# Attention ahead of a mixture of experts: the turns of the queries and outputs a step later, the first twelve weight decodes in four pinned parts, a reordered start

## Chip, cores and metric

The kernel runs on one core of a Trainium2 chip. The metric is the device time of one execution in microseconds (us); the number to compare is the median of several runs. The engines are PE (matrix products, with PEld for its weight loads), DVE (vector), ACT (activation functions and copies), POOL (GpSimd) and SP, which here issues transfers (DMA).

## What is computed

Three stages follow one another; the change touches the first and the preparation of the second.

```python
def phi(x):                                # x: 8 batches, 8 heads, 576 rows, 64
    proj = np.einsum('bhsd,df->bhsf', x, w_phi)          # 128 features
    proj = proj - np.max(np.abs(proj), axis=-1, keepdims=True)
    return np.concatenate([np.exp(proj), np.exp(-proj)], axis=-1)
q_p, k_p = (phi(q), phi(k))
kv = np.einsum('bhsf,bhsd->bhfd', k_p, v)
z = np.sum(k_p, axis=2)
num = np.einsum('bhsf,bhfd->bhsd', q_p, kv)
den = np.einsum('bhsf,bhf->bhs', q_p, z)[..., None] + 1e-06
attn = num / den
h = x @ w_in                               # x: 4608 tokens x 512 from attn; 2048 hidden
x1 = (h * np.cos(h)) @ w_out
# then 8 experts, each token through the one of its largest logit (relu between w1 and w2)
```

The weights of the FFN (the second stage) arrive as 64-bit floats in two 32-bit words each, and the kernel itself turns a piece of 128 x 512 into 32-bit values: this is called a decode here.

## The kernel before

**Items and steps.** The attention works on 16 items (j = 0 to 15), each two batches by two heads. An item has five steps (m = 0 to 4), which cover 2, 2, 1, 2 and 2 blocks of 128 tokens of its rows. A step is written out as `turns(j,m)` and then `products(j,m)`, and runs as a software pipeline over two items: the projections belong to item j, the outputs to item j-1, the transposes of the loaded rows to item j+1.

**turns(j,m)** issues, on PE, the transposes `pt` of item j+1's rows (L110; ACT copies them to kT or qT, L113), the transposes `ptt` of the centred query features t_q of one step earlier (`qexp`, L178; ACT makes the two exponentials qx from them, L184), and the turn `po` of finished outputs xs of one step earlier, item j-1 (`outT`, L215; ACT copies them to xo, L217, and the last step of an item issues their transfer, L220). Then ACT makes the keys' exponentials ke (`kexp`, L142 and L143). At m = 1 and 2 the loads of later items are issued on SP's queue.

**products(j,m)** issues, on PE, the projections `pj` of queries and keys (L125), the outputs' numerators and denominators `pn` of item j-1 (`num`, L199), and the sums `kv` over the keys of two steps earlier (L163; at m = 4 ahead of pj). DVE then does, in this order of the code: m_q and t_q (the maximum and the difference, L130 and L131), rd (L204, L205) and xs (L206) of `num`, kvz (a copy of kv, L169, in some steps), m_k and t_k.

**What sets the order.** PE's instructions keep the written order (`keep`). DVE, ACT, POOL and SP are put in order by a scheduler, except for instructions that are kept in program order. `pj` has one tile of two banks; pt and ptt share two tiles, po and pn another two, kv two more.

**Decodes.** `moes` drives the attention as a generator with 170 stops, two per step, and calls other work between them; the stops 15 to 149 are run by one loop. In that loop a decode is called once per item, at n % 10 == 2 for items 3 to 14, which is m = 1: Abs on ACT (L398), four operations on DVE (L399, L400, L402, L403), a cast on ACT (L404), a subtraction on POOL (L408), and the staging transfer of the next piece into the single tile `sx` (L377 to L380). A scheduler is free to move these. Further decodes are called in the last 20 stops and in the FFN.

Of the kernel before, what the change touches and what calls it, by code (L numbers as in the profile page):

```python
# [11 lines left out]
F32 = mybir.dt.float32  # L12
# [3 lines left out]
AF = mybir.ActivationFunctionType  # L16
ALU = mybir.AluOpType
# [3 lines left out]
P = 128  # L21
# [4 lines left out]
F32_MAX = float.fromhex("0x1.dffffep-96")  # L26


def f32(ap):
    return ap.bitcast(F32)  # L30
# [13 lines left out]
def attention(tc, ctx, S, ps, ident, q, k, v, w_phi, xt):  # L44

    nc=tc.nc
    keep=tc.keep_in_program_order
    D=64; F=128; E1=D+1
    raw=ctx.enter_context(tc.tile_pool(name="a_raw",bufs=2))
    ap=ctx.enter_context(tc.tile_pool(name="a_sb",bufs=2))  # L50
# [1 line left out]
    pp=pctx.enter_context(tc.tile_pool(name="a_ps",bufs=1,space=PSUM))  # L52

    w2=ap.tile([P,F],F32,name="w2",bufs=1)
    for s in range(2): nc.sync.dma_start(w2[s*D:(s+1)*D,:],w_phi)
    nc.scalar.preload_act_table_set("natural_log_exp_and_others")

    items=[(bp,hp) for bp in range(4) for hp in range(4)]
    NI=len(items)
# [11 lines left out]
    def load_v(i):  # L71
        bp,hp=items[i]
        r=raw.tile([P,2,9,E1],F32,tag="vh",name=f"v_{i}")
        nc.gpsimd.memset(r[:,:,:,D:E1],1.0)
        for bb in range(2):
            s=v[2*bp+bb,2*hp:2*hp+2]
            for h in range(2):
                nc.sync.dma_start(r[:,h,5*bb:5*bb+4,0:D], s[h,0:512,:].rearrange("(p c) d -> p c d",c=4))
            nc.sync.dma_start(r[64*bb:64*bb+64,:,4,0:D], s[:,512:576,:].rearrange("h p d -> p h d"))
        return r  # L80

    raws={}
    def ld(t,i):
        if i<NI: raws[t,i]=load_v(i) if t=="v" else load(t,{"k":k,"q":q}[t],i)
# [3 lines left out]
    def block(r,b):  # L88
        r,r2=r
        if b==4: return r2.rearrange("p h d -> p (h d)")  # L90
        if b>4: b-=1
        j,h=b//2,b%2
        return r[:,h,2*j:2*j+2,:].rearrange("p c d -> p (c d)")
# [9 lines left out]
    def turn(i,m):  # L103
        pt=ps.tile([P,512],F32,tag="tr",name=f"pt_{i}_{m}")
        c=0; made=[]
        for t,c0,n in TURN[m]:
            if (t,i) not in T: T[t,i]=S("xT",f"{t}T_{i}")
            a=c
            for b in range(c0,c0+n):
                keep(nc.tensor.transpose(pt[:,c*P:(c+1)*P], block(raws[t,i],b), ident)); c+=1  # L110
            made.append((T[t,i][:,c0*P:(c0+n)*P],pt[:,a*P:c*P]))
        def vec():
            for x,p in made: nc.scalar.copy(x,p)  # L113
        return vec
# [72 lines left out]
    xss={}; xos={}  # L187
    def num(i,g):

        n=GR[g][1]; t0=GR[g][0]  # L190
        x=qx.pop((i,g))
        pn=ps.tile([P,512],F32,tag="nm",name=f"pn_{i}_{g}")
        for t in range(n):
            for h in range(2):
                o=pn[:,(2*t+h)*E1:(2*t+h+1)*E1]
                for sg in range(2):
                    for c in range(2):
                        bb=c if t0+t==4 else int(t0+t>4)
                        keep(nc.tensor.matmul(o[64*c:64*c+64],x[:,h,sg,t*P+64*c:t*P+64*c+64],kvs[i,bb][:,2*h+sg,:],start=sg==0,stop=sg==1,skip_group_check=True))  # L199
        pv=pn[:,:2*n*E1].rearrange("p (g d) -> p g d",d=E1)  # L200
        xs=xss[i,g]=ap.tile([P,256],F32,tag="xs",name=f"xs_{i}_{g}")
        def vec():
            r=ap.tile([P,4,1],F32,tag="rd",name=f"rd_{i}_{g}")[:,:2*n,:]
            nc.vector.tensor_scalar(r,pv[:,:,D:E1],1e-6,None,op0=ALU.add)  # L204
            nc.vector.reciprocal(r,r)  # L205
            nc.vector.tensor_tensor(xs[:,:n*P].rearrange("p (g d) -> p g d",d=D),pv[:,:,0:D],r.to_broadcast([P,2*n,D]),ALU.mult)  # L206
        return vec
# [15 lines left out]
    def at(j,m): return divmod(5*j+m,5)  # L223
    def turns(j,m):

        vecs=[]
        if j+1<NI: vecs.append(turn(j+1,m))
        i,g=at(j,m-1)
        if 0<=i<NI: vecs.append(qexp(i,g))
        i,g=at(j-1,m-1)  # L230
        if 0<=i<NI: vecs.append(outT(i,g))
        for f in vecs: f()
        i,g=at(j,m-1)
        if 0<=i<NI: kexp(i,g)
        if m==1:
            for t in "kq": ld(t,j+2)
        if m==2 and j>0: ld("v",j+1)
    def products(j,m):
# [11 lines left out]
        if todo and g==4: kvfin(i,1)  # L250
        if vk: vk()
        if j==NI-1 and m==4: pctx.close()
    for i in range(2):
        for t in "kqv": ld(t,i)
    for m in range(5): turn(0,m)()
    for j in range(NI+1):
        for m in range(5):
            turns(j,m)
            yield
            products(j,m)  # L260
            yield
    turns(NI+1,0)


def gate_consts(tc, ctx, cpool, ps, ident, modality_id, modality_bias, w_gate, wgt):
# [62 lines left out]
def moes(tc, ctx, consts, S, ps, ident, att, end_att, xt, w_in, w_out, x1d, tab, wgt, w1, w2, out):  # L328

    nc=tc.nc  # L330
# [3 lines left out]
    turns={}  # L334
    def turn(tags,what):

        n=turns.get(what,0); turns[what]=n+1
        return tags[n%len(tags)]
# [31 lines left out]
    def stage():  # L370

        x=next(sq,None)
        if x is None: return
        f,which=x
        a=stg(f"st_{f}_{which}")
        if which==0:
            nc.sync.dma_start(a.rearrange("p (c f) -> p c f",c=4),win64[:,:,f*P:(f+1)*P,:].rearrange("p c f w -> p c (f w)"))  # L377
        else:
            nc.sync.dma_start(a,wout64[f*P:(f+1)*P,:])
        st[f,which]=a  # L380
    decoded=[0]
    parts=[]
    def decode(paced=False):

        x=next(todo,None)
        if x is None: return
        decoded[0]+=1
        f,which=x
        v=st[f,which].rearrange("p (f w) -> p f w",w=2)
        H=v[:,:,1]; L=v[:,:,0]  # L390
        t=xtile("gl" if decoded[0]<=17 else "row",f"d_t{which}_{f}",F32)
        ti=t.bitcast(I32)
        h,l=pair(wtag[which][f],f"w{which}_{f}")
        (win,wout)[which][f]=(h,l)
        keep=tc.keep_in_program_order if paced else lambda ins: ins
        def one():

            nc.scalar.activation(t,H.bitcast(F32),AF.Abs,scale=2.0**-112)  # L398
            keep(nc.vector.tensor_scalar(t,t,F32_MAX,None,op0=ALU.min))  # L399
            keep(nc.vector.tensor_scalar(ti,ti,3,None,op0=ALU.logical_shift_left))  # L400
        def two():
            keep(nc.vector.scalar_tensor_tensor(ti,L,29,ti,op0=ALU.logical_shift_right,op1=ALU.bitwise_or))  # L402
            keep(nc.vector.scalar_tensor_tensor(ti,H,-0x80000000,ti,op0=ALU.bitwise_and,op1=ALU.bitwise_or))  # L403
            nc.scalar.copy(h,t)  # L404
            stage()
        def three():
            if paced: keep(nc.vector.tensor_tensor(l,t,f32(h),ALU.subtract))  # L407
            else: nc.gpsimd.tensor_tensor(l,t,f32(h),ALU.subtract)  # L408
        if paced: parts.append([one,two,three])
        else:  # L410
            one(); two(); three()
    def decode_part(n):
# [266 lines left out]
    def keep(ins):  # L679

        if pin: tc.keep_in_program_order(ins)
# [134 lines left out]
    for n in range(15,170-TAIL):  # L816
        next(att)

        if n%10==2 and 3<=n//10<15: decode()
    head={0:[lambda:load_x(0),stage],11:[lambda:split_x(0,0),lambda:split_x(0,1)],12:[lambda:split_x(0,2)],13:[lambda:split_x(0,3),lambda:step(0)],  # L820
          15:[lambda:step(1)],17:[lambda:step(2)]}
    for n in (1,5,10,12,15,17): head.setdefault(n,[]).append(lambda: decoded[0]<len(early) and decode())
# [171 lines left out]
```

## Time and profile before

| | us |
|---|---|
| median of 3 runs | 1741.84 |
| lowest and highest | 1739.44, 1741.93 |
| profiled execution | 1744.49 |
| its span | 1742.8 |
| mean granted clock of PE | 0.986 |

The profile is of one execution, whose own time lies 2.65 above the median and 1.7 above its span. Over the whole span PE is busy 94%, its weight loads 80%, DVE 66%, ACT 48%, POOL 24%. These shares are means over three unlike stages. The attention takes the first 415.69 us of the span, up to the first product of the FFN.

In the timelines a row starts with the time from the span's start, then the duration, the engine, the line of the code, the operation, what it writes and reads, and in brackets how long the engine had been idle and what ended that. Rows of several instructions of one kind are drawn together (x32).

### The profile page before, as it was taken

How to read it: one execution, taken by the hardware profiler on the slowest of the kernel's cores; microseconds unless marked ns; L12 is line 12 of the kernel's file. 1: busy time of each engine (PE TensorE's matmuls, PEld its weight loads, DVE VectorE, ACT ScalarE, POOL GpSimd, SP SyncE). 2: the span in 40 equal slices, each digit the busy share in tenths (PEclk: the TensorE clock that was granted, in tenths of full speed). 3: DMA queues.
4: the chain of work that ended last, by engine and by line, in shares of the span. 5: the costliest groups of instructions: out<-in, count | busy, mean ns of one | idle time of the engine just before them, and what ended most of it. 6: DMA issues, size and time to landing. Idle time of an engine off the chain costs nothing.

```text
span 1742.8 us, 33504 instructions
## 1 busy us (share of the span) xinstructions
PE 1637.3 (94%) x13058; PEld 1388.5 (80%) x13058; DVE 1144.7 (66%) x2332; ACT 830.5 (48%) x1529; POOL 426.4 (24%) x351
## 2 busy tenths in 40 slices
PE   6888999888979999999999999999799999999997
PEld 5777787777758888888888888878678999899976
DVE  3877666677886676768676868664556565655645
ACT  4566555555443343434343434344336565655645
POOL 0110000002232343433333334352321221211112
PEclk9999999999999999999999999999899999999999
DMA  6443333341321010101010101000358775766656
GB/s 182 139 152 116 101 111 97 106 130 54 111 86 64 13 37 12 38 7 43 7 43 7 43 7 43 7 1 25 122 158 330 238 241 183 250 226 218 224 182 211
DMA packets 142544, 190.06 MB, mean 109 GB/s; under 512 B 64535, under 2 KB 89239, under 8 KB 142370
## 3 DMA queue, kind: packets, MB, share of 16 engines
q1 hardware_dynamic: 134578, 166.74, 30.3%
q0 software_dynamic: 7792, 21.02, 3.6%
q8 instruction: 108, 1.77, 0.4%
q14 instruction: 66, 0.54, 0.1%
HBM read 157.98 MB, written 30.51 MB: 108 GB/s over the span
## 4 chain that ended last, share of the span: by engine, by line
PE 68%; DVE 16%; issue 6%; DMA 5%; ACT 3%; SPq 1%; POOL 1%; another core or an unknown queue 0%; DVEq 0%; POOLq 0%; ACTq 0%
PE ph L444 18%; PE acc L478 14%; PE mh L728 11%; PE po L740 10%; PE pj L125 4%; PE acc L483 4%; PE pn L199 2%; DMA tab<-rec,pi 2%; PE kv L163 2%; DVE m_q L130 1%; DVE t_q L131 1%; DVE t_k L131 1%; DVE d_t L403 1%; DVE m_k L130 1%; DVE x L434 1%
## 5 line engine op out<-in xcount | busy, mean ns | idle before, releaser
L444 PE MATMUL ph<-x,w 128*128 128x512 f32 x1728 | 424.0, 393 | 11.3 <-DVE fr L464 5.9
L444 PEld LDWEIGHTS ph<-x,w 128*128 128x128 f32 x1728 | 322.7, 188 | 87.1 <-DVE fr L464 8.2
L467 POOL TENSOR_TENSOR gl<-fr,gh 128x512 fp32r<-128x512 f32 x144 | 217.9, 1515 | 437.7 <-DVE gh L466 374.0
L688 DVE TENSOR_TENSOR m<-raw,m 128x512 fp32r<-128x512 f32 x320 | 210.3, 694 | 141.5 <-ACT m L687 141.0
L478 PE MATMUL acc<-w,gh 128*128 128x512 f32 x896 | 277.5, 391 | 1.9 <-DVE w L407 1.4
L687 ACT CAST m<-raw 128x512 fp32r<-128x512 f32 x320 | 187.0, 618 | 70.3 <-PE mh L728 33.6
L728 PEld LDWEIGHTS mh<-xT,m 128*128 128x128 f32 x1728 | 212.2, 194 | 7.1 <-DVE hl L731 3.7
L728 PE MATMUL mh<-xT,m 128*128 128x256 f32 x1728 | 213.3, 285 | 4.6 <-DVE hl L731 3.3
L457 ACT ACTIVATE n<-ph 128x512 int32<-128x512 f32 x144 | 85.8, 596 | 265.2 <-PE ph L444 264.8
L478 PEld LDWEIGHTS acc<-w,gh 128*128 128x128 f32 x896 | 169.0, 189 | 37.6 <-DVE w L407 1.7
L459 DVE SCALAR_TENSOR_TENSOR fr<-ph,n 128x512 f32<-128x512 f32 x144 | 99.1, 689 | 145.6 <-ACT n L457 131.6
L740 PE MATMUL po<-m,hh 128*128 128x512 f32 x576 | 181.3, 396 | 1.8 <-ACT hh L730 1.8
L508 DVE SCALAR_TENSOR_TENSOR junk<-x1T,wg 128x512 f32<-128x512 f32 x224 | 180.9, 808 | 0.0
L478 PE MATMUL acc<-w,gl 128*128 128x512 f32 x448 | 174.8, 390 | 0.0
L461 ACT ACTIVATE fr<-fr 128x512 f32<-128x512 f32 x144 | 91.1, 633 | 150.4 <-DVE fr L459 149.7
L464 DVE SCALAR_TENSOR_TENSOR fr<-fr,ph 128x512 f32<-128x512 f32 x144 | 98.7, 685 | 66.8 <-ACT fr L462 66.8
L740 PEld LDWEIGHTS po<-m,hh 128*128 128x128 f32 x576 | 106.0, 190 | 22.2 <-ACT hh L730 2.2
L778 POOL DMA_INDIRECT out_dram<-o,mrec x39 | 43.6, 1118 | 293.1 <-ACT o L777 284.8
L130 DVE TENSOR_REDUCE m_q<-pj 128x4 f32<-128x512 f32 (+1 forms) x80 | 50.9, 636 | 96.4 <-PE pj L125 96.4
L740 PE MATMUL po<-m,hl 128*128 128x512 f32 x288 | 113.1, 393 | 0.1
L478 PEld LDWEIGHTS acc<-w,gl 128*128 128x128 f32 x448 | 84.4, 188 | 17.7
L462 ACT ACTIVATE fr<-fr 128x512 f32<-128x512 f32 x144 | 91.0, 632 | 4.3
(189 smaller groups left out, 2364.9 us busy)
## 6 DMA issues: line engine op xcount, KB each, us to landing
raw<-in_moe_w_dram SPq DMA_DIRECT2D x171, 512.0 KB, 6.3
xt<-xo SPq DMA_DIRECT2D x16, 576.0 KB, 2.9
xr<-xt SPq DMA_DIRECT2D x36, 256.0 KB, 2.8
raw_k<-in_k_dram SPq DMA_DIRECT2D x32, 256.0 KB, 3.1
raw_q<-in_q_dram SPq DMA_DIRECT2D x32, 256.0 KB, 3.3
v<-in_v_dram SPq DMA_DIRECT2D x64, 128.0 KB, 3.0
st<-in_moe_w_in_dram SPq DMA_DIRECT2D x16, 512.0 KB, 3.7
st<-in_moe_w_out_dram SPq DMA_DIRECT2D x16, 512.0 KB, 3.6
```

Of the source, the lines that this page charges most:

```text
L444: nc.tensor.matmul(ph,A[:,ws],xhl[u,d][k],start=n[0]==0,stop=n[0]==11); n[0]+=1
L459: nc.vector.scalar_tensor_tensor(g,ph,INV2PI,n,op0=ALU.mult,op1=ALU.subtract)
L461: nc.scalar.activation(g,g,AF.Sin,scale=math.pi)
L462: nc.scalar.activation(g,g,AF.Square)
L464: nc.vector.scalar_tensor_tensor(g,g,-0.5,ph,op0=ALU.add,op1=ALU.mult)
L467: nc.gpsimd.tensor_tensor(gl,g,f32(gh),ALU.subtract)
L478: nc.tensor.matmul(accs[u][c],A[:,ws],B,start=(f==0 and k==0),stop=(f==NF-1 and k==2))
L508: return lambda: tc.keep_in_program_order(nc.vector.scalar_tensor_tensor(junk,x1T[u,c],1.0,wg[e],op0=ALU.mult,op1=ALU.mult,accum_out=lgs[u ...
L687: keep(nc.scalar.copy(h,a))
L688: keep(nc.vector.tensor_tensor(l,a,f32(h),ALU.subtract))
L728: nc.tensor.matmul(ph[:,f2*T:(f2+1)*T],A[:,ws],B[d//2][:,xs],start=n==0,stop=n==11); n+=1
L740: nc.tensor.matmul(po[c],A[:,ws],B,start=(f==0 and j==0),stop=(f==NF2-1 and j==2))
```

## The change

Four things are changed.

- `qexp` and `outT` are issued one step later: at step m they take what was made two steps earlier, not one. xs gets three buffers instead of two, and one more step of turns is added after the last item.
- The twelve decodes of the loop are cut into four parts, at the stops n, n+2, n+4 and n+6, which follow `turns(j,1)` to `turns(j,4)`. Each part has one operation of DVE, kept in program order: Abs and L415 in the first, L416, L417, then L418 with the cast, the staging transfer and POOL's subtraction.
- Item 1's first transposes are spread differently over item 0's steps: none at m = 0, then 0, 1, 2 with 3, and 4.
- The load of w_phi (w2) moves behind the first load of k.

```diff
@@ -52,7 +52,6 @@
     pp=pctx.enter_context(tc.tile_pool(name="a_ps",bufs=1,space=PSUM))
 
     w2=ap.tile([P,F],F32,name="w2",bufs=1)
-    for s in range(2): nc.sync.dma_start(w2[s*D:(s+1)*D,:],w_phi)
     nc.scalar.preload_act_table_set("natural_log_exp_and_others")
 
     items=[(bp,hp) for bp in range(4) for hp in range(4)]
@@ -198,7 +197,7 @@
                         bb=c if t0+t==4 else int(t0+t>4)
                         keep(nc.tensor.matmul(o[64*c:64*c+64],x[:,h,sg,t*P+64*c:t*P+64*c+64],kvs[i,bb][:,2*h+sg,:],start=sg==0,stop=sg==1,skip_group_check=True))
         pv=pn[:,:2*n*E1].rearrange("p (g d) -> p g d",d=E1)
-        xs=xss[i,g]=ap.tile([P,256],F32,tag="xs",name=f"xs_{i}_{g}")
+        xs=xss[i,g]=ap.tile([P,256],F32,tag="xs",name=f"xs_{i}_{g}",bufs=3)
         def vec():
             r=ap.tile([P,4,1],F32,tag="rd",name=f"rd_{i}_{g}")[:,:2*n,:]
             nc.vector.tensor_scalar(r,pv[:,:,D:E1],1e-6,None,op0=ALU.add)
@@ -224,10 +223,10 @@
     def turns(j,m):
 
         vecs=[]
-        if j+1<NI: vecs.append(turn(j+1,m))
-        i,g=at(j,m-1)
+        for n in ((),(0,),(1,),(2,3),(4,))[m] if j==0 else (m,) if j+1<NI else (): vecs.append(turn(j+1,n))
+        i,g=at(j,m-2)
         if 0<=i<NI: vecs.append(qexp(i,g))
-        i,g=at(j-1,m-1)
+        i,g=at(j-1,m-2)
         if 0<=i<NI: vecs.append(outT(i,g))
         for f in vecs: f()
         i,g=at(j,m-1)
@@ -250,8 +249,10 @@
         if todo and g==4: kvfin(i,1)
         if vk: vk()
         if j==NI-1 and m==4: pctx.close()
-    for i in range(2):
-        for t in "kqv": ld(t,i)
+    ld("k",0)
+    for s in range(2): nc.sync.dma_start(w2[s*D:(s+1)*D,:],w_phi)
+    ld("q",0); ld("v",0)
+    for t in "kqv": ld(t,1)
     for m in range(5): turn(0,m)()
     for j in range(NI+1):
         for m in range(5):
@@ -259,7 +260,7 @@
             yield
             products(j,m)
             yield
-    turns(NI+1,0)
+    for m in range(2): turns(NI+1,m)
 
 
 def gate_consts(tc, ctx, cpool, ps, ident, modality_id, modality_bias, w_gate, wgt):
@@ -381,6 +382,8 @@
     decoded=[0]
     parts=[]
     def decode(paced=False):
+        for _ in decoding(paced): pass
+    def decoding(paced=False,steps=False):
 
         x=next(todo,None)
         if x is None: return
@@ -406,7 +409,15 @@
         def three():
             if paced: keep(nc.vector.tensor_tensor(l,t,f32(h),ALU.subtract))
             else: nc.gpsimd.tensor_tensor(l,t,f32(h),ALU.subtract)
-        if paced: parts.append([one,two,three])
+        if steps:
+            keep=tc.keep_in_program_order
+            keep(nc.scalar.activation(t,H.bitcast(F32),AF.Abs,scale=2.0**-112))
+            yield keep(nc.vector.tensor_scalar(t,t,F32_MAX,None,op0=ALU.min))
+            yield keep(nc.vector.tensor_scalar(ti,ti,3,None,op0=ALU.logical_shift_left))
+            yield keep(nc.vector.scalar_tensor_tensor(ti,L,29,ti,op0=ALU.logical_shift_right,op1=ALU.bitwise_or))
+            keep(nc.vector.scalar_tensor_tensor(ti,H,-0x80000000,ti,op0=ALU.bitwise_and,op1=ALU.bitwise_or))
+            keep(nc.scalar.copy(h,t)); stage(); three()
+        elif paced: parts.append([one,two,three])
         else:
             one(); two(); three()
     def decode_part(n):
@@ -816,7 +827,8 @@
     for n in range(15,170-TAIL):
         next(att)
 
-        if n%10==2 and 3<=n//10<15: decode()
+        if n%10==2 and 3<=n//10<15: work=decoding(steps=True)
+        if n>=32 and n%2==0: next(work,None)
     head={0:[lambda:load_x(0),stage],11:[lambda:split_x(0,0),lambda:split_x(0,1)],12:[lambda:split_x(0,2)],13:[lambda:split_x(0,3),lambda:step(0)],
           15:[lambda:step(1)],17:[lambda:step(2)]}
     for n in (1,5,10,12,15,17): head.setdefault(n,[]).append(lambda: decoded[0]<len(early) and decode())
```

Line numbers after differ by one in the attention (L109, L124, L177, L198, L214 for L110, L125, L178, L199, L215); the parts of the decode are L414 to L419.

On PE, step (8,1), before: the names carry the item and the step (po_7_0 is the turn of xs of item 7, step 0).

```order
L110 MATMUL pt_9_1_3289<-ident_60,raw_k_9_2914 128x128 x4
L178 MATMUL ptt_8_0_3294<-ident_60,t_q_8_0_3239 128x128 x4
L215 MATMUL po_7_0_3301<-ident_60,xs_7_0_3262 128x128 x2
L125 MATMUL pj_8_1_3334<-w2_87,qT_8_2996 128x128 x4
L125 MATMUL pj_8_1_3334<-w2_87,kT_8_2815 128x128 x4
L199 MATMUL pn_7_1_3345<-kvz_7_0_3206,qx_7_1_3003 64x65 x16
```

The same step after:

```order
L109 MATMUL pt_9_1_3276<-ident_60,raw_k_9_2901 128x128 x4
L177 MATMUL ptt_7_4_3281<-ident_60,t_q_7_4_3163 128x128 x4
L214 MATMUL po_6_4_3287<-ident_60,xs_6_4_3186 128x128 x2
L124 MATMUL pj_8_1_3314<-w2_87,qT_8_2976 128x128 x4
L124 MATMUL pj_8_1_3314<-w2_87,kT_8_2803 128x128 x4
L198 MATMUL pn_7_1_3325<-kvz_7_0_3194,qx_7_1_3059 64x65 x16
```

The transposes ptt and the turn po of the step before have given place to those of two steps before; the projection pj_8_1 stands behind them as it did.

On DVE, step (1,4) before, with one of the twelve decodes (d_t0_2) in it:

```order
L169 COPY kvz_1_0_835<-kv_1_0_669 128x260
L399 TENSOR_SCALAR d_t0_2_2132<-d_t0_2_2132 128x512
L400 TENSOR_SCALAR d_t0_2_2132<-d_t0_2_2132 128x512
L130 TENSOR_REDUCE m_q_1_4_828<-pj_1_4_799 128x4
L402 SCALAR_TENSOR_TENSOR d_t0_2_2132<-st_2_0_1743,d_t0_2_2132 128x512
L131 TENSOR_TENSOR t_q_1_4_804<-pj_1_4_799,m_q_1_4_828 128x512
L204 TENSOR_SCALAR rd_0_4_831<-pn_0_4_810 128x4
L130 TENSOR_REDUCE m_k_1_4_837<-pj_1_4_799 128x4
L205 RECIPROCAL rd_0_4_831<-rd_0_4_831 128x4
L403 SCALAR_TENSOR_TENSOR d_t0_2_2132<-st_2_0_1743,d_t0_2_2132 128x512
L206 TENSOR_TENSOR xs_0_4_827<-pn_0_4_810,rd_0_4_831 128x256
L131 TENSOR_TENSOR t_k_1_4_809<-pj_1_4_799,m_k_1_4_837 128x512
```

The same kind of place after, step (8,1), with a first and a second part of a decode:

```order
L129 TENSOR_REDUCE m_q_8_1_3359<-pj_8_1_3314 128x4
L130 TENSOR_TENSOR t_q_8_1_3319<-pj_8_1_3314,m_q_8_1_3359 128x512
L415 TENSOR_SCALAR d_t0_4_3310<-d_t0_4_3310 128x512
L203 TENSOR_SCALAR rd_7_1_3362<-pn_7_1_3325 128x4
L129 TENSOR_REDUCE m_k_8_1_3368<-pj_8_1_3314 128x4
L204 RECIPROCAL rd_7_1_3362<-rd_7_1_3362 128x4
L168 COPY kvz_7_1_3366<-kv_7_1_3150 128x260
L205 TENSOR_TENSOR xs_7_1_3342<-pn_7_1_3325,rd_7_1_3362 128x256
L130 TENSOR_TENSOR t_k_8_1_3324<-pj_8_1_3314,m_k_8_1_3368 128x512
L416 TENSOR_SCALAR d_t0_4_3310<-d_t0_4_3310 128x512
```

Before, the scheduler put all four operations of a decode into one step of an early item, among m_q, t_q and xs. After the change, L415 stands between t_q and rd of the step (8,1), L416 behind its t_k, and the other two parts in the next two steps.

On PE, the start before:

```order
L110 MATMUL pt_0_4_156<-ident_60,raw_q_0_97 128x128 x4
L110 MATMUL pt_1_0_162<-ident_60,raw_k_1_111 128x128 x4
L125 MATMUL pj_0_0_169<-w2_87,qT_0_146 128x128 x4
L125 MATMUL pj_0_0_169<-w2_87,kT_0_132 128x128 x4
L110 MATMUL pt_1_1_186<-ident_60,raw_k_1_111 128x128 x4
L178 MATMUL ptt_0_0_191<-ident_60,t_q_0_0_174 128x128 x4
L125 MATMUL pj_0_1_215<-w2_87,qT_0_146 128x128 x4
```

And after:

```order
L109 MATMUL pt_0_4_156<-ident_60,raw_q_0_97 128x128 x4
L124 MATMUL pj_0_0_162<-w2_87,qT_0_146 128x128 x4
L124 MATMUL pj_0_0_162<-w2_87,kT_0_132 128x128 x4
L109 MATMUL pt_1_0_179<-ident_60,raw_k_1_111 128x128 x4
L124 MATMUL pj_0_1_201<-w2_87,qT_0_146 128x128 x4
L124 MATMUL pj_0_1_201<-w2_87,kT_0_132 128x128 x4
L109 MATMUL pt_1_1_218<-ident_60,raw_k_1_111 128x128 x4
L177 MATMUL ptt_0_0_223<-ident_60,t_q_0_0_167 128x128 x4
```

The first transposes of item 1 (pt_1_0) stood ahead of the first projection and now stand behind it; ptt_0_0 is a step later.

## Rows read from the trace of the kernel before

**Rows 1.** Windows: length, busy (count) of PE, PEld, DVE, ACT, POOL, PEclk, DMA, GB/s

```profile
100.00:125.00 25.00, 20.86 (x372) 18.09 (x372) 19.29 (x45) 17.00 (x37) 3.89 (x4) 0.95 0.53 157
200.00:250.00 50.00, 45.49 (x891) 39.70 (x891) 32.28 (x78) 28.57 (x66) 0.26 (x2) 1.00 0.37 107
```

**Rows 2.** Timeline, DVE, items 7 to 8: start, us, engine, line, operation [idle <-releaser]

```profile
201.09 0.69 DVE L130 TENSOR_REDUCE m_q<-pj 128x4 f32<-128x512 f32 x1 [1.70 <-PE pj L125]
...
205.40 0.43 DVE L130 TENSOR_REDUCE m_q<-pj 128x2 f32<-128x256 f32 x1 [0.90 <-PE pj L125]
...
214.79 0.69 DVE L130 TENSOR_REDUCE m_q<-pj 128x4 f32<-128x512 f32 x1 [0.54 <-PE pj L125]
...
219.69 0.69 DVE L130 TENSOR_REDUCE m_q<-pj 128x4 f32<-128x512 f32 x1 [1.70 <-PE pj L125]
...
221.88 0.69 DVE L131 TENSOR_TENSOR t_k<-pj,m_k 128x512 f32<-128x512 f32 x1
222.49 0.41 DVE L206 TENSOR_TENSOR xs<-pn,rd 128x256 f32<-128x256 f32 x1
224.59 0.69 DVE L130 TENSOR_REDUCE m_q<-pj 128x4 f32<-128x512 f32 x1 [1.69 <-PE pj L125]
```

**Rows 3.** Timeline, PE, the same place: two waits of the turned outputs

```profile
218.14 0.41 PE L215 MATMUL po<-ident,xs 128*128 128x128 f32 x2 [1.16 <-ACT qx L184]
...
223.05 0.41 PE L215 MATMUL po<-ident,xs 128*128 128x128 f32 x2 [0.36 <-DVE xs L206]
```

**Rows 4.** Timeline, PEld, one step: weight loads of each product

```profile
219.57 1.01 PEld L199 LDWEIGHTS pn<-kvz,qx 128*64 128x64 f32 x32
220.50 1.02 PEld L163 LDWEIGHTS kv<-v,ke 128*64 128x64 f32 x32
221.59 0.42 PEld L110 LDWEIGHTS pt<-ident,raw_k 128*128 128x128 f32 x4
221.98 0.47 PEld L178 LDWEIGHTS ptt<-ident,t_q 128*128 128x128 f32 x4
223.01 0.20 PEld L215 LDWEIGHTS po<-ident,xs 128*128 128x128 f32 x2 [0.57 <-ACT kT L113]
223.38 0.52 PEld L125 LDWEIGHTS pj<-w,qT 64*128 64x128 f32 x8 [0.17 <-issue]
```

**Rows 5.** Timeline, ACT: a decode's first operation in item 2; an exponential of (8,0)

```profile
88.92 0.67 ACT L398 ACTIVATE d_t<-st 128x512 f32<-128x512 f32 x1
...
224.51 0.65 ACT L143 ACTIVATE ke<-t_k 128x512 f32<-128x512 f32 x1
```

**Rows 6.** Timeline, DVE, the decode of item 2

```profile
89.63 0.43 DVE L399 TENSOR_SCALAR d_t<-d_t 128x512 f32<-128x512 f32 x1 [0.72 <-ACT d_t L398]
```

**Rows 7.** Timeline, PE, a wait behind that decode

```profile
92.46 0.63 PE L178 MATMUL ptt<-ident,t_q 128*128 128x128 f32 x4 [1.39 <-DVE rd L204]
```

**Rows 8.** Page, DMA issues: count, KB each, us to landing

```profile
st<-in_moe_w_in_dram SPq DMA_DIRECT2D x16, 512.0 KB, 3.7
```

**Rows 9.** Timeline, PE, start: first projection and the transposes ahead of it

```profile
14.64 1.08 PE L110 MATMUL pt<-ident,raw_k 128*128 128x128 f32 x4 [2.82 <-DMA raw_k<-in_k_dram]
15.65 1.23 PE L125 MATMUL pj<-w,qT 64*128 64x128 f32 x8
```

**Rows 10.** Timeline, DVE, first m_q of steps (0,0), (1,1), (2,0), (13,0), (15,0), (15,4)

```profile
17.78 0.69 DVE L130 TENSOR_REDUCE m_q<-pj 128x4 f32<-128x512 f32 x1 [14.94 <-PE pj L125]
...
47.42 0.69 DVE L130 TENSOR_REDUCE m_q<-pj 128x4 f32<-128x512 f32 x1
...
70.19 0.69 DVE L130 TENSOR_REDUCE m_q<-pj 128x4 f32<-128x512 f32 x1 [2.26 <-PE pj L125]
...
337.54 0.69 DVE L130 TENSOR_REDUCE m_q<-pj 128x4 f32<-128x512 f32 x1 [1.70 <-PE pj L125]
...
388.86 0.69 DVE L130 TENSOR_REDUCE m_q<-pj 128x4 f32<-128x512 f32 x1 [1.70 <-PE pj L125]
...
407.45 0.69 DVE L130 TENSOR_REDUCE m_q<-pj 128x4 f32<-128x512 f32 x1 [0.54 <-PE pj L125]
```

## Prediction

> **What bounds the kernel now.** I read the stretches of the span first, then the timelines of DVE, PE and the weight loads in one item of the attention, then the waits behind a decode, and last the start. The order of instructions differs only in the attention, which ends with the first product of the FFN about 416 us into the span, and in the ten microseconds behind it; everything after that stands as before. So the whole prediction is about the sixteen items of five steps each.
>
> In the quiet middle (items 5 to 11) no engine is full: of 50 us PE is busy 45.49, its weight loads 39.70, DVE 32.28, ACT 28.57, at clock 1.00 [rows 1]. The reader should see that the stretch is bounded by a loop and not by an engine. The loop shows when the starts of m_q are laid beside each other [rows 2]: step (8,0) begins at 219.69, its t_k ends at 221.88 + 0.69 = 222.57, its xs at 222.49 + 0.41 = 222.90, and only then, at 223.05, can PE turn that xs (po waits 0.36 for it, its weight load sat idle 0.57) [rows 3, 4]. The projection of the next step stands behind po on PE, begins at 223.38 [rows 4], and m_q of (8,1) follows 1.21 us later at 224.59 [rows 2]. PE thus waits for the last DVE operation of each step, and then DVE waits 1.69 for PE. One item takes 224.59 - 201.09 = 23.50 us [rows 2].
>
> **The moved turns.** After the change po turns, and ptt transposes, what DVE finished a whole step earlier, so neither has anything to wait for; the same instructions are issued as often as before. What still ties a step to the one before is that there is one tile pj: its products need t_k of the previous step to have read it. A step therefore takes the longer of two: PE's own work, or DVE from m_q to the end of t_k (2.88), the release (0.15, as from the end of xs to po), and projection to m_q (1.21), together 4.24. Since pj is single, the slack of one step can't be given to the next, and the item is the sum of the longer ones:
> - m = 0 to 1: 4.90 before; without the idle 0.57 it is 4.33, just over DVE's 4.24.
> - m = 1 to 2: 205.40 - 201.09 = 4.31. DVE also copies kvz here ahead of t_k, so DVE's chain is the longer one already; unchanged, 4.31.
> - m = 2 to 4: 214.79 - 205.40 = 9.39 for both. The wait before po of the second one (as long as in the first step) goes: 8.82. The one-token po and ptt move from the second to the first of the two, which shifts work between them and changes nothing in their sum.
> - m = 4 to 0: 219.69 - 214.79 = 4.90. Here po waited 1.16 [rows 3]; whichever ended last, the exponentials that the row names or xs, both are a step old afterwards. Without the wait PE has the shorter way, and DVE's 4.24 decides.
>
> Together 4.33 + 4.31 + 8.82 + 4.24 = 21.70 us, 1.80 less than 23.50. That a row names another releaser (the copy of kT for the idle weight load) does not matter here, since that copy too is older than po.
>
> **The decodes.** Items 2 to 14 take 388.86 - 70.19 = 318.67 us [rows 10], 13.2 more than 13 x 23.50 = 305.5; that excess is what decodes cost now. They stand at the wrong place: three to four DVE operations in one step, between m_q, t_q and xs, and PE behind them waits up to 1.39 [rows 7]. After the change each item from 3 to 14 has one decode, with one DVE operation in a step. Three of the four come behind t_k or xs, in time in which DVE would wait for pj (0.5 to 1.7 per step now [rows 2], less later), and I cost these at nothing; should that cover be gone, each costs at most its own duration, 0.4 to 0.7. The first one, L415, is pinned between t_q and rd of m = 1, hence ahead of t_k, in the step in which DVE's chain is the longer. It also waits for Abs on ACT, which stands behind the second exponential of the keys. That one ends at 224.51 + 0.65 = 225.16, Abs takes 0.67 and ends at 225.83 [rows 5]. With the quicker step m_q of (8,1) is at 224.02, t_q ends 1.42 later at 225.44: DVE waits about 0.4, and the operation takes 0.43 [rows 6], of which some 0.06 overlaps with its neighbours as all of DVE's rows do. That is 0.80 per decode, and 22.50 for such an item. Bounds: nothing, when Abs comes earlier and the operation is hidden, and 1.39, the longest wait behind a decode now. I stay near the middle because both durations come from rows.
>
> Items 13 and 14 hold four more decodes without pins: 388.86 - 337.54 = 51.32, or 4.3 over two quiet items [rows 10]. They are bunched up after the change by the order of DVE; I take 6, from 4 (as now) to 8 (twice).
> Items 2 to 14: 21.70 + 12 x 22.50 + 6 = 297.7, a gain of 21.0 (11.9 with 1.39 and 8; 32.6 with nothing and 4).
>
> **The start.** pj of (0,0) begins at 15.65 behind item 1's first transposes, which waited 2.82 for their load until 14.64 [rows 9]. Moved behind it, pj is free for as much as 3 us earlier. Later the constants' DVE work waits for its small loads, up to (1,1) at 47.42, and those loads are issued by SP in a row; much of the gain is lost there. Bounds 0 and 3.2, taken 2.0. From (1,1) to (2,0) it is 70.19 - 47.42 = 22.77 [rows 10]; without hoisted decodes it is 21.70 - 4.33 = 17.37, so 5.4 (3.5 if part of that is the loads). The load of w_phi now stands behind raw_k's first, still ahead of q, which pj needs in any case.
>
> **The end.** Item 15's first four steps take 407.45 - 388.86 = 18.59 [rows 10]. Without transposes of a next item (0.42 each [rows 4]) m = 2 to 4 is 8.82 - 0.84 = 7.98: 4.24 + 4.31 + 7.98 = 16.53, a gain of 2.1 (at least 1). One step of turns is added at the end and one wait for xs goes; with the FFN's first products behind it I take 0, up to 2 of gain.
>
> **Sum.** 2.0 + 5.4 + 21.0 + 2.1 = 30.5 us. The profiled run took 1744.49; so 1714.0 in its terms. That run is 2.65 above the median of 1741.84, so the median becomes 1711.3. The low bounds add to 16.4 (1725.4).
>
> **Rivals.**
> A. The pinned operation costs nothing (ACT is less than 60% busy [rows 1], so Abs may come early enough). Then 12 x 0.80 = 9.6 more: 1744.5 - 40.1 - 2.65 = 1701.7. Against it: the five ACT operations ahead of Abs run back to back after pt's end. Chance 0.10.
> B. The granted clock falls. While decodes were in the items it was 0.95 (100 to 125 us), in the middle, with its 1.16 waits once an item, 1.00 [rows 1, 3]. 0.95 means a tenth of the stretch at 1.2 GHz instead of 2.4 GHz, hence 2.5 of 25 us at half speed and 1.25 lost. If the one longer wait for L415 in each of twelve items does this, 1.15 x 12 = 13.8 goes: gain 16.7, time 1725.1. The same time comes if the wait for xs is merely replaced by that for t_k, which ends 0.33 earlier. Chance of either 0.17. [...]
> C. Slower: the pin turns a late load into a stall. L415 waits for Abs, Abs for the staging load (512 KB, 3.7 us to landing [rows 8]), which uses a single tile and is issued after the previous decode's last read, behind loads of q in SP's queue. DVE can no longer go round it: t_k, xs and then PE stand behind. This decides from 30.5 / 12 = 2.5 us per decode beyond the 0.80; with 4 us it is 48 lost, 1744.5 + 17.5 - 2.65 = 1759. Against it: from that last read to the next Abs there are at least two steps (4.24 + 4.33 = 8.6 us), some 4.9 more than the landing. Chance 0.06.
> D. Nothing changes: the waits of PE are replaced in full by equally long ones in the single pj. About 1742. Against it: DVE's 4.24 is from its own rows. Chance 0.04. Something between B and D 0.03.
>
> **How the numbers follow.** The forecast (gains of 25 to 36) has 0.60. The range takes in A, the low bounds and B: 1701 to 1728, leaving out 0.13. About 0.2% (3.5 us) is what a measurement of this kernel can tell from no change: faster 0.60 + 0.10 + 0.17 + 0.03 = 0.90, same 0.04, slower 0.06.
>
> **What would show it.** In the changed profile, quiet items 21.7 us long and those with a decode 22.5; po's waits for xs gone, and instead short waits of pj for t_k; L415 with a wait of about 0.4 for Abs and the rest of the decode hidden; (2,0) near 62.8; the FFN begins near 385. If po still waits, or items 5 to 11 are as long as now, the loop was not what I take it for; if L415 waits microseconds, it is C; if the clock is below 1.00 between 150 and 330 us, it is B.

## The result, and the profile after

The changed kernel takes 1710.3 us (median of 4, 1708.39 to 1711.51) against 1741.88 in the same set of runs: a ratio of 0.9818, 95% interval 0.9801 to 0.9835, 28.7 to 34.7 us faster. Forecast were 1711 and a gain of 30.5. The profiled execution took 1708.39, with a span of 1706.3.

The page of the changed kernel, its span and the busy time of PE and PEld:

```profile
span 1706.3 us, 33457 instructions
...
PE 1618.9 (95%) x13058; PEld 1384.3 (81%) x13058; DVE 1145.9 (67%) x2332; ACT 829.2 (49%) x1529; POOL 427.7 (25%) x351
```

The windows of after that answer to [rows 1] (length, busy time and count of PE, PEld, DVE, ACT, POOL, then clock, DMA share, GB/s):

```profile
100.00:125.00 25.00, 22.94 (x444) 20.84 (x442) 19.41 (x47) 16.35 (x39) 1.41 (x2) 1.00 0.43 122
200.00:250.00 50.00, 45.29 (x902) 40.96 (x900) 37.76 (x93) 33.58 (x77) 2.96 (x5) 1.00 0.46 140
```

The first stretch, which held hoisted decodes before, now has clock 1.00 and PE busy 22.94 instead of 20.86. In the second, which held none before and now holds about two, PE's own row hardly moves (45.29 against 45.49); the gain shows in its weight loads, 40.96 against 39.70. DVE's rise, 37.76 against 32.28, is mostly the decodes' own operations, which take 4.83 us there.

The timeline of DVE in items 8 and 9 after, the lines that answer to [rows 2]:

```profile
197.14 0.69 DVE L129 TENSOR_REDUCE m_q<-pj 128x4 f32<-128x512 f32 x1 [1.01 <-PE pj L124]
...
201.50 0.69 DVE L129 TENSOR_REDUCE m_q<-pj 128x4 f32<-128x512 f32 x1 [1.15 <-PE pj L124]
...
206.56 0.42 DVE L129 TENSOR_REDUCE m_q<-pj 128x2 f32<-128x256 f32 x1 [0.57 <-PE pj L124]
...
215.37 0.69 DVE L129 TENSOR_REDUCE m_q<-pj 128x4 f32<-128x512 f32 x1 [0.53 <-PE pj L124]
...
219.59 0.69 DVE L129 TENSOR_REDUCE m_q<-pj 128x4 f32<-128x512 f32 x1 [1.01 <-PE pj L124]
...
221.78 0.69 DVE L130 TENSOR_TENSOR t_k<-pj,m_k 128x512 f32<-128x512 f32 x1
...
223.95 0.69 DVE L129 TENSOR_REDUCE m_q<-pj 128x4 f32<-128x512 f32 x1 [1.15 <-PE pj L124]
...
225.68 0.43 DVE L415 TENSOR_SCALAR d_t<-d_t 128x512 f32<-128x512 f32 x1 [0.32 <-ACT d_t L414]
...
229.00 0.42 DVE L129 TENSOR_REDUCE m_q<-pj 128x2 f32<-128x256 f32 x1 [0.56 <-PE pj L124]
```

The starts of m_q give the steps of item 8: 4.36 from 197.14 to 201.50, 5.06 to 206.56, 8.81 for the two to 215.37, 4.22 to 219.59; 22.45 in all. L415 waited 0.32 for Abs and took 0.43, in the middle of the chain to t_k. On PE, at the start of item 9 (answering to [rows 3]):

```profile
218.39 0.72 PE L124 MATMUL pj<-w,qT 64*128 64x128 f32 x8 [0.74 <-DVE t_k L130]
...
222.43 0.38 PE L214 MATMUL po<-ident,xs 128*128 128x128 f32 x2
222.74 0.71 PE L124 MATMUL pj<-w,qT 64*128 64x128 f32 x8
...
226.56 0.38 PE L214 MATMUL po<-ident,xs 128*128 128x128 f32 x2
228.25 0.49 PE L124 MATMUL pj<-w,qT 64*128 64x128 f32 x4 [1.30 <-DVE t_k L130]
```

po has no wait any more, at 222.43 nor at 226.56. PE waits at pj instead, for t_k: 0.74 at m = 4 to 0, 1.30 at m = 1 to 2, and not at all in the other steps (pj at 222.74 follows po at once). The waits between 100 and 300 us (engine, line, for what: us in total, times, longest) have no row of po left:

```profile
DVE m_q L129 <- PE pj L124: 40.3, 44, 1.4
...
PE pj L124 <- DVE t_k L130: 18.4, 18, 1.3
...
DVE d_t L415 <- ACT d_t L414: 2.8, 9, 0.3
```

The starts of the same steps as in [rows 10]: (0,0), (1,1), (2,0), (13,0), (15,0), (15,4):

```profile
14.09 0.69 DVE L129 TENSOR_REDUCE m_q<-pj 128x4 f32<-128x512 f32 x1 [11.25 <-PE pj L124]
...
45.59 0.68 DVE L129 TENSOR_REDUCE m_q<-pj 128x4 f32<-128x512 f32 x1
...
63.17 0.69 DVE L129 TENSOR_REDUCE m_q<-pj 128x4 f32<-128x512 f32 x1 [1.01 <-PE pj L124]
...
309.38 0.69 DVE L129 TENSOR_REDUCE m_q<-pj 128x4 f32<-128x512 f32 x1 [1.01 <-PE pj L124]
...
357.16 0.68 DVE L129 TENSOR_REDUCE m_q<-pj 128x4 f32<-128x512 f32 x1
...
374.89 0.69 DVE L129 TENSOR_REDUCE m_q<-pj 128x4 f32<-128x512 f32 x1 [0.54 <-PE pj L124]
```

### The profile page after: what moved, and what is told of

Read it like the earlier page. It is cut to its first block, busy times and chain, and to the rows that moved or that the text cites. A ratio compares the mean times of both kernels' runs of the same rounds, so it can differ in the third digit from the quotient of the medians.

```text
span 1706.3 us, 33457 instructions
## 1 busy us (share of the span) xinstructions
PE 1618.9 (95%) x13058; PEld 1384.3 (81%) x13058; DVE 1145.9 (67%) x2332; ACT 829.2 (49%) x1529; POOL 427.7 (25%) x351
## 4 chain that ended last, share of the span: by engine, by line
PE 72%; DVE 13%; issue 5%; DMA 5%; ACT 4%; SPq 1%; POOL 1%; another core or an unknown queue 0%; DVEq 0%; POOLq 0%; ACTq 0%
PE ph L455 19%; PE acc L489 15%; PE mh L739 11%; PE po L751 10%; PE acc L494 4%; PE pj L124 3%; PE kv L162 3%; PE pn L198 2%; DMA tab<-rec,pi 2%; PE pt L109 2%; DVE x L445 1%; DMA raw<-in_moe_w_dram 1%; DVE t_k L130 1%; DVE d_t L406 1%; DVE m_k L129 1%
```

## The experiments

Each kernel below is timed beside the kernel before on the same chip; a ratio is to that. Differences between two of them come from these ratios, and the intervals of the single ratios are 4 to 11 us wide, so the step lengths of the traces, which in regular items repeat within 0.02 almost everywhere, tell more than the totals. They are differences of the starts of m_q, here of a regular item between 6 and 10:

| kernel | 0 to 1 | 1 to 2 | 2 to 4 | 4 to 0 | item | time, us | ratio (95%) |
|---|---|---|---|---|---|---|---|
| before | 4.90 | 4.31 | 9.39 | 4.91 | 23.51 | 1741.9 | 1 |
| after | 4.36 | 5.06 | 8.81 | 4.22 | 22.45 | 1710.3 | 0.9818 (0.9801-0.9835) |
| turns_only | 4.36 | 4.31 | 8.81 | 4.23 | 21.71 | 1717.1 | 0.9840 (0.9824-0.9857) |
| parts_only | 4.91 | 5.09 | 9.29 | 4.91 | 24.20 | 1738.5 | 0.9962 (0.9949-0.9975) |
| outt_only | 4.36 | 5.06 | 8.81 | 4.22 | 22.45 | 1711.4 | 0.9798 (0.9775-0.9822) |
| qexp_only | 4.90 | 5.11 | 9.51 | 4.90 | 24.42 | 1742.3 | 0.9984 (0.9973-0.9995) |
| late415 | 4.36 | 4.31 | 8.81 | 4.22 | 21.70 | 1700.8 | 0.9754 (0.9726-0.9783) |
| tkfirst | 4.36 | 4.47 | 8.81 | 4.22 | 21.87 | 1702.7 | 0.9763 (0.9737-0.9789) |
| late_tkall | 4.36 | 3.79 | 8.82 | 4.15 | 21.12 | 1692.9 | 0.9701 (0.9670-0.9733) |
| late_tkall_tail | 4.36 | 3.79 | 8.82 | 4.15 | 21.12 | 1689.4 | 0.9690 (0.9663-0.9717) |
| quad415 | 4.37 | 6.25 | 8.81 | 4.22 | 23.65 | 1728.4 | 0.9921 (0.9899-0.9943) |

**The parts of the change, one at a time.** The theory is that of the prediction; the first rival holds the decodes' places to be the larger part.

> The kernel before with the two moves of turns alone; decodes free and bunched in early items as before, start as before. Theory: items without decodes 21.7 us instead of 23.5 (items 6 to 12), the bunched ones keep their excess of about 9 us; gain 1.8 x 14.5 = 26 less what bunched decodes take back, time 1716 to 1722. Rival (the decodes' places are the larger part): 1730 or more.

The quiet items came out at 21.70 to 21.71, all the gain of the loop without the rest of the change, and the time in the range given. Items 1 to 5, in which the scheduler still put the decodes, took 27.28, 25.07, 26.98, 27.04 and 23.15.

> The kernel before with the twelve pinned decodes alone. Theory: quiet items stay at 23.5, an item with a decode about 24.3 since L415 lies in DVE's chain at m = 1 too; it wins the excess of the bunched decodes (about 14 over items 1 to 4) and pays 0.8 to 1.2 twelve times: gain 0 to 5, time 1737 to 1742. Rival (bunching was the larger part): gain over 10, 1731 or less.

The pinned decodes alone win 6.6 us (0.38%), a little more than expected. Items 3 to 13 are 24.2 long: L415 costs 0.8 in the step 1 to 2 with the old turns as with the new, and the other three operations cost nothing (the other steps are as long as before or 0.1 shorter). The two ratios fall by 0.0160 and 0.0038; the change as a whole by 0.0182. The moved turns are the larger part; whether the parts add up to the whole can't be told within these intervals.

**Which of the two turns.** The changed kernel with one of the two put back to its old place, so that the other alone is a step later:

```diff
         # outt_only
-        i,g=at(j,m-2)
+        i,g=at(j,m-1)
         if 0<=i<NI: vecs.append(qexp(i,g))
```

```diff
         # qexp_only
-        i,g=at(j-1,m-2)
+        i,g=at(j-1,m-1)
         if 0<=i<NI: vecs.append(outT(i,g))
```

> The changed kernel, but the transposes of the queries' features (qexp) stay one step back as before; only the turned outputs (outT) are moved. Theory (the wait of po for xs, at the end of DVE's step, held the loop): the whole gain stays, items with a decode 22.5 us, items without 21.7, time about 1710. Rival (the exponentials were what po and the products waited for): the 1.16 wait at m = 4 to 0 stays, item 23.1 or more, time about 1720.

> The changed kernel, but the turned outputs (outT) stay one step back as before; only qexp is moved. Theory: po waits for xs again, 0.57 and 0.57 and 0.7 more per item, item with a decode 24.3 us, time about 1737 (1710 + 15 x 1.8). Rival (the exponentials held the loop): half or more of the gain stays, 1724 or less.

With outT alone every item from 2 on is as long as with both (within 0.02); with qexp alone the loop is the old one (24.42 beside the 24.20 of parts_only). In qexp_only's waits between 100 and 300 us po stands as before, behind xs in 16 of its steps, by its row behind the exponentials in 8, and by its row behind the copy of qT in 8 more:

```profile
PE po L214 <- DVE xs L205: 10.7, 16, 1.0
PE po L214 <- ACT qx L183: 10.3, 8, 1.3
...
PE po L214 <- ACT qT L112: 4.0, 8, 0.5
```

In outt_only, whose exponentials stand where they were, all three rows are gone, and PE has only its wait for t_k:

```profile
DVE m_q L129 <- PE pj L124: 38.5, 44, 1.2
...
PE pj L124 <- DVE t_k L130: 17.3, 18, 1.3
```

So the row that named the exponentials (the 1.16 of [rows 3]) was not about them: leaving them in place and moving xs ended the wait. The time of qexp_only lies 5 above what was expected; its item 14, with decodes that the scheduler bunched there, took 28.48 us, against 24.37 before.

**L415, and what stands ahead of t_k.** late415 moves L415 to the next part; tkfirst writes t_k ahead of the output's operations at m = 1; late_tkall does both, the second in every step:

```diff
-            yield keep(nc.vector.tensor_scalar(t,t,F32_MAX,None,op0=ALU.min))
-            yield keep(nc.vector.tensor_scalar(ti,ti,3,None,op0=ALU.logical_shift_left))
+            yield
+            yield keep(nc.vector.tensor_scalar(t,t,F32_MAX,None,op0=ALU.min))
+            keep(nc.vector.tensor_scalar(ti,ti,3,None,op0=ALU.logical_shift_left))
...
         if vq: vq()
+        if vk: vk()
         if vn: vn()
         if todo and g==2: kvfin(i,0)
         if todo and g==4: kvfin(i,1)
-        if vk: vk()
```

> The changed kernel with the first DVE operation of each decode taken out of the chain of m = 1: Abs alone in the first part, L415's operation one part later (behind t_k), the next two together, the last as it was. Theory: step 1 to 2 falls from 5.05 to 4.31, 0.74 x 12 = 8.9 less than the changed kernel, about 1701.5. Rival (DVE's work as such costs the time, wherever it stands): other steps grow by as much, about 1710.

> The changed kernel with t_k written ahead of kvz and xs at m = 1 only. Theory (t_k frees the single pj, so what stands ahead of it is paid in full): kvz (0.31) and xs (0.33) leave the chain, step 1 to 2 falls by 0.64 in some 15 items, 9.5 in all, about 1701. Rival (the step is held by PE, or xs late now holds pn): unchanged, about 1710.

> Both at once, and t_k ahead of rd, kvz and xs in every step. Theory: the step 1 to 2 becomes PE's (about 3.75), 4 to 0 loses about 0.1; item with a decode 22.45 - 1.30 - 0.1 = 21.0, about 20 less than the changed kernel, 1690. Rival (the freed time is taken by the next wait, xs for pn or ACT's copies): half of it, 1700.

The step 1 to 2 fell to 4.31 in late415, to the number, and in items 3 to 13 no other step grew. Item 14, with the bunch of decodes that have no pins, did: 27.32 there and 27.06 in tkfirst, against 25.34 in the changed kernel. In tkfirst the step 1 to 2 fell by 0.59 of the 0.64 expected. With both it is 3.79, with no wait of PE in it, and the item 21.12 instead of 21.0; the one wait of PE that is left is 0.67 in the step 4 to 0. DVE in late_tkall_tail, from m_q to the next m_q, step (7,1):

```profile
172.89 0.69 DVE L129 TENSOR_REDUCE m_q<-pj 128x4 f32<-128x512 f32 x1 [0.80 <-PE pj L124]
...
174.22 0.68 DVE L129 TENSOR_REDUCE m_k<-pj 128x4 f32<-128x512 f32 x1
...
175.00 0.69 DVE L130 TENSOR_TENSOR t_k<-pj,m_k 128x512 f32<-128x512 f32 x1
...
175.70 0.40 DVE L168 COPY kvz<-kv 128x260 f32<-128x260 f32 x1
176.01 0.41 DVE L205 TENSOR_TENSOR xs<-pn,rd 128x256 f32<-128x256 f32 x1
176.34 0.41 DVE L416 TENSOR_SCALAR d_t<-d_t 128x512 f32<-128x512 f32 x1
176.67 0.42 DVE L129 TENSOR_REDUCE m_q<-pj 128x2 f32<-128x256 f32 x1
```

t_k starts 2.11 after m_q, where after L415, kvz and xs it started 3.47 after it (227.42 against 223.95 in the changed kernel). kvz, xs and the decode's operation now lie in the time in which PE works on.

> The same, and the decodes behind the twelve (the last twenty stops) also cut in parts, one per stop, instead of left to the scheduler, which bunched five of them in items 14 and 15. Theory: items 14 and 15 lose their excess of 2.9 + 1.2, 3 to 4 less than without, 1687. Rival (the FFN's first products then wait for their weights): the gain is given back, 1690 or more.

In the changed kernel the decodes behind the twelve (L402 to L406) stand together in items 14 and 15, beside the last pinned one, and DVE has no wait left there (changed kernel, DVE, around the steps (14,2) and (14,3)):

```profile
340.59 0.75 DVE L402 TENSOR_SCALAR d_t<-d_t 128x512 f32<-128x512 f32 x2
341.26 0.42 DVE L403 TENSOR_SCALAR d_t<-d_t 128x512 int32<-128x512 int32 x1
341.60 0.41 DVE L129 TENSOR_REDUCE m_q<-pj 128x2 f32<-128x256 f32 x1
...
343.91 0.68 DVE L405 SCALAR_TENSOR_TENSOR d_t<-st,d_t 128x512 int32<-128x512 int32 x1
...
344.85 0.68 DVE L406 SCALAR_TENSOR_TENSOR d_t<-st,d_t 128x512 int32<-128x512 int32 x1
...
346.05 0.68 DVE L129 TENSOR_REDUCE m_q<-pj 128x4 f32<-128x512 f32 x1
```

Item 14 takes 25.34 there and 25.15 in late_tkall; with the late decodes cut in parts it takes 21.12, like the others. These decodes now stand in item 15 and behind it, and the excess of item 15 stays: its first four steps take 17.84, against 17.53 in late_tkall. The medians fell by 3.5, near what was expected, the ratios by 0.0011 (1.9 us); their intervals overlap, so the totals neither show the gain nor exclude the rival. PE of late_tkall_tail is busy 193 of 200 us and its loads 175, at clock 1.00:

```profile
100.00:300.00 200.00, 193.06 (x3827) 175.28 (x3825) 164.45 (x385) 137.53 (x311) 13.92 (x19) 1.00 0.48 139
```

This is the fastest version but for best_nest below, which can't be told from it: 0.9690 of the time before, 22 us below the changed kernel by the ratios (0.9818 - 0.9690, times 1742).

**The start.**

oldstart puts item 1's first transposes and the load of w_phi back; nest keeps the zeros' tiles while the constants are made:

```diff
         # oldstart
-        for n in ((),(0,),(1,),(2,3),(4,))[m] if j==0 else (m,) if j+1<NI else (): vecs.append(turn(j+1,n))
+        if j+1<NI: vecs.append(turn(j+1,m))
...
         # nest
-        return gate_consts(tc, ctx, cpool, ps, ident, modality_id, modality_bias, w_gate, wgt)
+            return gate_consts(tc, ctx, cpool, ps, ident, modality_id, modality_bias, w_gate, wgt)
```

> The changed kernel with the start as before: item 1's first transposes in their old places, w_phi loaded first. Theory of the prediction: the reordered start is worth about 2 of the 7.4 us that step (2,0) gained, so (2,0) comes near 65 instead of 63.2, time 1712. Rival (the constants' DVE work, which becomes ready at 39.5 in both traces, takes back the whole gain of the start): (0,0) at 17.8, but (2,0) within 0.5 of 63.2, time 1710.

(0,0) begins at 17.83 and (2,0) at 66.75, 3.6 later than in the changed kernel, and the FFN at 386.4 instead of 382.8. So the reordered start is worth 3.6 there, more than expected, and the rival is out. The total (0.9793, 0.9769 to 0.9818) doesn't show it: the two ratios' intervals overlap, and from the first ph, the FFN's first product, to the first mh, the experts' first, the profiled executions of the nine kernels with the same order of instructions there differ by up to 2.6 us (829.8 to 832.4; 830.8 after, 829.9 here). What the start is worth in the total stays open.

> The changed kernel with the tiles of the gate's constants in space of their own, instead of in the space of the zeros whose four transfers land at 39.2. Theory: POOL's first constant waits for these transfers to leave the space, DVE's casts wait for POOL, and t_q of (1,0) stands behind them (3.4 idle); without that (1,0) goes on at once and the small loads are issued some 4 us earlier, so (2,0) comes 3 to 5 earlier, at 58 to 60, time about 1706. Rival (item 1 is held by the loads for items 1 and 2 in SP's row): (2,0) stays within 1 of 63.2, time 1710.

Where the start's gain is lost is seen in the changed kernel at 35 to 41 us. On POOL the constants wait for the zeros to leave the space that they take over:

```profile
39.23 0.21 POOL L288 MEMSET tf<- 128x128 f32 x1 [36.06 <-DMA x1d<-zero]
```

and on DVE t_q stands behind the casts of these constants, 4.2 behind its m_q:

```profile
35.48 0.69 DVE L129 TENSOR_REDUCE m_q<-pj 128x4 f32<-128x512 f32 x1 [1.35 <-PE pj L124]
39.55 0.17 DVE L294 CAST rev<-ri 128x8 f32<-128x8 int32 x1 [3.38 <-POOL ri L293]
...
39.72 0.68 DVE L130 TENSOR_TENSOR t_q<-pj,m_q 128x512 f32<-128x512 f32 x1
```

nest took that wait away, and the step (1,1) came a microsecond earlier, at 44.56, but (2,0) came at 63.43: the theory's price was wrong. The rival's number came true, but its reason, the loads in SP's row, is not shown by that. On PE the time was lost again (nest, PE):

```profile
48.11 0.49 PE L124 MATMUL pj<-w,qT 64*128 64x128 f32 x4 [2.47 <-DVE t_k L130]
...
48.75 1.14 PE L198 MATMUL pn<-kvz,qx 128*64 128x65 f32 x16
49.67 1.95 PE L162 MATMUL kv<-v,ke 128*64 128x65 f32 x32
```

PE had waited 2.47 for t_k, and the rows after it are at the lower clock: pn 1.14 for 16 products where 0.69 is usual, kv 1.95 where it is 1.10. The granted clock was 0.78 between 50 and 55 us. The changed kernel has such a wait one step earlier, with the lower clock behind it (granted 0.73 between 40 and 45 us). Its row names g, a DVE operation that ends 0.1 behind t_k:

```profile
42.36 1.22 PE L124 MATMUL pj<-w,qT 64*128 64x128 f32 x8 [2.30 <-DVE g L279]
```

There nest waits 0.48 and its clock is 1.00. It thus moved the wait and the fall one step on: its PE is 2.9 ahead at the next transposes (44.07 against 46.98) and level at the ones after (51.55 against 51.58). The total is 1706.9 (0.9785, 0.9762 to 0.9807), which can't be told from the changed kernel.

> The fastest so far (t_k first in every step, L415 out of the chain, the late decodes in parts) with the constants in space of their own as well. Theory: the gains lie at different places and add, 1689 - 4 = 1685. Rival (the earlier start is taken back at item 2's loads): 1689.

1687.65, ratio 0.9673 (0.9651 to 0.9695), beside 0.9690 (0.9663 to 0.9717): no difference that can be told; (2,0) is at 62.47 and 62.80.

**A longer wait of PE in each item.**

```diff
+            for _ in range(3): keep(nc.vector.tensor_scalar(t,t,F32_MAX,None,op0=ALU.min))
             yield keep(nc.vector.tensor_scalar(t,t,F32_MAX,None,op0=ALU.min))
```

> The changed kernel with the first DVE operation of each decode done four times instead of once (repeating it changes nothing in the values), so that three more of about 0.34 stand ahead of t_k at m = 1 and PE waits there some 1.0 longer, 2.3 in all. Theory (every operation ahead of t_k is paid once, in full): step 1 to 2 is 6.1, twelve items 12 longer in all, 1722 or 1723, clock 1.00 in items 3 to 12. Rival B of the prediction (a wait that returns in each item makes PE's clock fall): the granted clock between 100 and 300 us falls below 1.00 and more than 24 are lost, 1735 or more.

Both were half right: the clock did fall, to 0.97 between 100 and 300 us, but not in every item, and the time is 5 to 6 above the theory's. The step 1 to 2 grew from 5.06 to 6.25, 0.40 for each added operation (the scheduler set them among rd, kvz and xs and m_k behind them all), and eight of the twelve items are 23.64 or 23.65 long. Items 8, 9 and 12 took 26.50, 25.14 and 24.97; item 14 has its bunch besides. PE behind the wait in item 7 and in item 8 (start, us, [idle]):

```profile
189.93 0.49 PE L124 MATMUL pj<-w,qT 64*128 64x128 f32 x4 [2.50 <-DVE t_k L130]
...
191.09 1.10 PE L162 MATMUL kv<-v,ke 128*64 128x65 f32 x32
...
213.58 0.80 PE L124 MATMUL pj<-w,qT 64*128 64x128 f32 x4 [2.50 <-DVE t_k L130]
...
215.66 1.95 PE L162 MATMUL kv<-v,ke 128*64 128x65 f32 x32
```

The wait is 2.50 both times; the kv behind it takes 1.10 in the one and 1.95 in the other. The windows behind the wait of item 7 and behind that of item 8, the clock third from the end:

```profile
190.00:195.00 5.00, 5.00 (x100) 4.52 (x102) 3.04 (x10) 3.49 (x8) 0.00 (x0) 1.00 0.39 86
215.00:220.00 5.00, 5.00 (x60) 4.55 (x60) 2.44 (x8) 1.46 (x3) 0.00 (x0) 0.51 0.15 32
```

1.00 against 0.51, hence nearly all of the second stretch at 1.2 GHz. By the row, waits of 1.30 in twelve items never brought the clock down in the changed kernel (1.00 from 50 to 350 us); waits of 2.50 did so in three of the eleven items before the bunch. The items pay 12 x 1.20 = 14.4 and 2.85 + 1.49 + 1.32 = 5.7 for the three; together 20, measured 18 (0.9921 - 0.9818).

## Why the prediction was right

**The loop.** It was taken for a loop through one tile, in which a step is the longer of PE's work and DVE's way to t_k. Four of its numbers can be read off: 4.33, 4.31, 8.82 and 4.24 forecast, 4.36, 4.31, 8.81 and 4.23 in turns_only, 21.70 for both. That t_k and not DVE's work as such holds the step is shown by late415 (the same operations, behind t_k, cost nothing in items 3 to 13) and by quad415 (three more ahead of it are paid in full). outt_only shows that only one of the two moved pieces did it; the prediction had not separated them.

**The decodes.** 0.80 for L415 was forecast (its own terms, 0.4 and 0.43 less 0.06, add to 0.77), 0.75 measured (22.45 against 21.70), made of a wait of 0.32 for Abs, where about 0.4 was said, and the operation. The other three at nothing: 8.81 and 4.22 are the same with and without them.

**Items 2 to 14.** 357.16 - 63.17 = 294.0 us where 297.7 was forecast. The step that was mis-sized is the bunch of late decodes: 6 was taken for items 13 and 14, and item 14's excess over 22.45 is 2.9, item 13's none. But item 15 was to have its first four steps in 16.53 and took 17.73: the bunch reaches into it (turns_only, whose bunch came earlier, has 16.47). Bunch and item 15 together: 2.9 + 1.2 against 6.

**The start.** (2,0) at 62.8 was forecast and 63.17 measured, 7.0 earlier than before. By place the two terms were right: 2.0 up to (1,1) was 47.42 - 45.59 = 1.8, and 5.4 from there on was 22.77 - 17.58 = 5.2. By cause they were not: the second was put down to the moved turns and the missing decodes, as for a quiet item, but in oldstart, which has both, (1,1) comes at 47.91 and (2,0) at 66.75. The stretch takes 18.84 there, so 3.9 of the 5.2 is theirs and 1.3 is the reordered start's, which gives 2.3 up to (1,1) and 3.6 in all. Of the 3.4 by which oldstart's (2,0) lies ahead of before, the turns alone give 3.2 (67.00 in turns_only) and the pinned decodes alone 2.1 (68.07 in parts_only): the two do not add. That the constants take back much of the start's gain was right ((0,0) 3.7 earlier, (1,1) 1.8), but the prediction named the small loads for it, and the trace has a wait of 3.38 for the zeros' space first, with 0.97 and 1.14 for two of those loads behind it; that the rest of item 1 would run like a quiet item without the reordered start was not right.

**The end.** The FFN begins at 382.8, 32.9 before the old 415.7. The profiled runs differ by 36.1 and the medians by 31.6; the 3 to 4 us that the profiled runs differ by behind the attention lie between the first ph and the first mh (834.9 before, 830.8 after). That may be more than scatter: the three kernels that turn the outputs in the old place (before, parts_only, qexp_only) have 833.3 to 834.9 there, and the nine kernels compared under "The start" above 829.8 to 832.4. What does it was not followed up.

**The total.** Up to (15,4) the traces gain 32.6, where 30.5 was forecast: 1.8 and 5.2 for the start, 24.7 for items 2 to 14, 0.9 for item 15, against 2.0, 5.4, 21.0 and 2.1. That the median came within 1.1 of the forecast gain is closer than these terms, and in part luck.

**The rivals.** A: Abs did not come earlier, the wait was there. B: not in this kernel, the clock is 1.00 in all decode items; quad415 shows it to lie not far off, at a wait of 2.50 instead of 1.30, and then only in some items. Its price of 1.15 per item does not follow from the 1.25 worked out ahead of it, which would make it 15.0 in all and 1726.3. The Trainium skill ("TensorE: Matmul & The Clock Gate", HAM oscillation) tells of a loop whose clock falls in every round, in each of which the products wait 3 to 5 us for a transfer. The waits here are shorter, so these rows do not test that: the clock fell behind none of twelve waits of 1.30 and behind three of eleven of 2.50. C: L415 waited 3.8 us in all twelve items together, 0.3 each; Abs never waited for its load. D: out, po's wait is not replaced in the steps 0 to 1 and 2 to 4.

## What to carry to other kernels

Where two engines hand one buffer to and fro, write out for each step which operation frees it, and put everything that the partner doesn't wait for behind that one: here xs, kvz and a decode's operation were worth 0.3 to 0.8 us each and item ahead of t_k, and nothing behind it. Work that is poured in from elsewhere was cheaper here when it was cut into pieces and pinned, one to a step (6.6 us in parts_only), than left to a scheduler, which put it in bunches; cutting and pinning were not tried apart. A row of waits names the releaser that came last by the trace; moving one suspect alone tells which it was.

## What the runs showed of the hardware

An equal wait of PE (2.50 us, with much the same work ahead of it) left items at their regular length, with the clock at 1.00, in eight cases and was followed by 1.2 GHz in three, where the same 32 products took 1.95 us in two cases and 1.52 in the third, instead of 1.10. So a wait of one length has two prices, 0 or 1.3 to 2.9 us beyond itself here; what decides between them the runs do not show. At 1.30 it was 0 in all twelve.

In the start, shortening one wait of PE (2.30 to 0.48 us between the changed kernel and nest) lengthened the next (0.80 to 2.47), and the lower clock moved with the longer wait. That this is why (2,0) doesn't move is read from one trace each, and no run keeps the clock up there to prove it.
